# A planned attention and feed-forward kernel: new costs in the planner, masks made on GpSimd, another order of the first loads, fewer idle products

## The chip, the core and the metric

The kernel runs on one core of one Trainium2 chip. The metric is the device time of one execution in microseconds (us). Names of engines: PE is TensorE (PEld its weight loads), DVE is VectorE, ACT is ScalarE, POOL is GpSimd, SP is SyncE, on whose queue every DMA of this kernel is issued.

## What is computed

Attention over 4 batches and 8 heads, 768 positions, 64 columns a head, with a window of 128 keys and the first 4 keys (sinks) always visible, then a feed-forward layer on the 3072 rows:

```python
scores = scale * np.matmul(q, k.transpose(0, 1, 3, 2))
keep = (pos[None, :] < n_sink) | ((rel >= 0) & (rel < window))
scores = np.where(keep, scores, -1e9)
a = np.exp(scores - np.max(scores, axis=-1, keepdims=True))
a = a / (np.sum(a, axis=-1, keepdims=True) + 1e-09)
x = np.matmul(a, v)                  # then heads side by side: 3072 x 512
h = x @ w_in                         # 512 x 2048
g = np.where(h > 0, h, np.exp(np.minimum(h, 0)) - 1)
out = g @ w_out                      # 2048 x 512
```

## The kernel before

**Tiles.** The 3072 rows are 24 tiles of 128, cut into nine chunks (`SIZES`): three of 2 tiles, then six of 3. One *visit* is one tile of queries with one pair of heads, so a chunk of 2 tiles has 8 visits, and visits are counted here from 0 through chunk 0 (0 to 7), chunk 1 (8 to 15), chunk 2 (from 16). A visit of the first tile of a batch sees one tile of keys (132 columns with the sinks), any other visit two (264).

**A visit.** *Scores* (PE, line 601 in the first three chunks, in f32; 595 and 596 later), *reduction* (DVE, 616: mask added and the row's minimum taken), *Exp* (ACT, 618, with the sum read back by an accumulator instruction), the small *eps* step (622, on POOL or ACT), reciprocal (DVE, 623). In chunk 0 then: a diagonal (POOL, 630), a *turn* on PE (636), its copy out of PSUM (640, on DVE or ACT) and the *values* product (PE, 653). From chunk 1 on: two f16 halves of the weights (ACT 668, DVE 669, the sinks on POOL 675 to 679), a DMA transpose (687), and the values product (701, 706). After the visits of a pair of heads, x is copied out of PSUM in two halves (the *x copy*: ACT 739, DVE 740). There is one PSUM bank for the values products, so the next pair's wait for the x copy.

**Feed-forward.** For each of 16 column blocks f: the *first product* (PE, 765, 12 matmuls), Exp on ACT (773), two steps of the elu (775 on DVE or POOL, 776 on DVE), a rounding copy on ACT (779), the rounding rest on POOL (786), and the *second product* (PE, 793). `PARTS` cuts chunk 0's blocks in two: first chunk 0 with f 0 to 6, then chunk 1 with f 0 to 12, then the rests. The first product of chunk 1 needs all four x copies of that chunk, the eighth counted from the start.

**Weights.** There are 32 pieces (2f for the first product, 2f+1 for the second). Each is loaded (314), opened on ACT (307) and DVE (308), rounded on ACT (456), and its rest is taken on POOL in two halves (457). They are converted while the first chunks run.

**The order.** Nothing is ordered by hand. `Plan` (line 104) holds tasks with an engine, a duration, a latency after it (`HOP`, and `lat` for DMAs) and the tasks they depend on. PE's tasks have a position; `backward` gives the others a due time, `forward` fills every engine by due time, and after `ROUNDS` rounds the best order is kept; `keep_order` then issues the instructions in it. So the durations given to `add` are what decides which instruction stands before which on ACT, DVE, POOL and SP. Each of these engines, and each queue, works in the order given, so an instruction that waits holds up those behind it.

**Idle products.** Where the plan sees PE idle for over `IDLE_LEAST` in its first `IDLE_UNTIL` us, `with_idle_products` puts matmuls in, whose result nothing reads (line 882; 29 of them).

**The start.** `spread` (1109) brings the two numbers n_sink and window to every partition by a product on PE (1111); `make_masks` (326) makes distances by an iota on POOL and four steps on DVE, then the masks (345, 348). The loads stand in the order n_sink, window, first keys, first values, second keys (1125 to 1136).

Of the kernel before, what the change touches and what calls it, by code (L numbers as in the profile page):

```python
# [52 lines left out]
IDLE_US, IDLE_FILL, IDLE_UNTIL, IDLE_LEAST = 0.11, 0.6, 100.0, 0.8  # L53
# [3 lines left out]
PE_T, PE_V = 0.25, 0.25  # L57
# [46 lines left out]
class Plan:  # L104


    HOP = {"PE": 0.15, "ACT": 0.08, "DVE": 0.08, "POOL": 0.2, "SP": 0.0}
# [176 lines left out]
def act_us(n, scaled=False):  # L284
    return 0.17 + 0.00088 * n + (0.08 if scaled else 0.0)


def dve_us(n):
    return 0.12 + 0.00115 * n


def pool_us(n):
    return 0.18 + 0.0019 * n
# [32 lines left out]
def make_masks(nc, tmp, sk, low, m0, m1, m2):  # L326


    ri = tmp[:, 0:P].bitcast(I32)
    rel, own, prev = (tmp[:, i * P : (i + 1) * P] for i in (1, 2, 3))  # L330
    nc.gpsimd.iota(ri, pattern=[[-1, P]], base=0, channel_multiplier=1)
    for j in range(NS):
        nc.gpsimd.memset(sk[:, j : j + 1], float(j))
# [32 lines left out]
def fast_path(tc, ctx, first, kq, vx, wt, out, low, spread, numbers, flag):  # L366
# [36 lines left out]
    spread(po_ps[0])  # L403
# [4 lines left out]
    tmp = pts[-1].rearrange("p b k -> p (b k)").bitcast(F32)  # L408
    second, rest = make_masks(nc, tmp[:, : 4 * P], tmp[:, 4 * P : 4 * P + NS], low, m0, m1, m2)
    nc.gpsimd.memset(ones, 1.0)  # L410
    for t in wu:
        nc.gpsimd.memset(t, 0)
    nc.gpsimd.memset(hot, 1.0)
    make_identity(nc, ident)
# [11 lines left out]
    second_ = add("DVE", 0.65, second)  # L426
    rest_ = add("DVE", 0.5, rest)
    numbers_ = add("DVE", 1.3, numbers)
# [12 lines left out]
    def weights(k):  # L441
# [3 lines left out]
        ld = add("SP", 0.4, lambda: load_weights(nc, raw, wt[k]), deps=[w_done.get(k - AHEAD, [None])[0]], lat=1.45)  # L445
        if wide:
            steps = weight_f32(nc, v, top, raw, 2.0)
            a = add("ACT", act_us(512), steps[0], deps=[ld])
            b = add("DVE", 0.13 + 0.00108 * 512, steps[1], deps=[a], slow=1.5)
# [45 lines left out]
    def attention(c):  # L495
# [12 lines left out]
        def split_keys(h):  # L508
# [4 lines left out]
            if c < DUP:  # L513
                ld = None
                if (c, h) not in first["kq"]:
                    ld = add("SP", 0.4, lambda: nc.sync.dma_start(st[:, :kw], kq[:, o : o + kw]), lat=dma_us(P * kw * 4) * 1.15)
                users = []
                return st, None, ld, ld, users
# [51 lines left out]
        for p in range(NP):  # L570
# [5 lines left out]
            for g in ts:  # L576
# [29 lines left out]
                else:  # L606
                    scs = [add("PE", 0.65, scores([0, 1]), deps=kqp[0][2:4], pos=at[k], line=1)] * 2
# [6 lines left out]
                for e in range(2):  # L614
                    ee, me = e3[:, e, :wd], mn[:, e : e + 1]
                    red = add("DVE", 0.24 + 0.001 * wd, lambda ee=ee, me=me, sp=sps[e], m=m, wd=wd, to_score=to_score: nc.vector.tensor_tensor_reduce(ee, sp[:, :wd], m[:, :wd], to_score, 3.0e38, ALU.add, ALU.min, me), deps=[scs[e], (None, second_)[t] if t < 2 else rest_])  # L616
# [263 lines left out]
    for writer, users in later:  # L880
        writer.deps.extend(users)
# [290 lines left out]
```

## Time and profile before

| | us |
|---|---|
| median of 3 executions | 627.38 (626.61 to 627.97) |
| the profiled execution | 628.19 |
| its span, first to last instruction | 626.3 |
| PE busy | 606.1 (97%) |
| first product of the feed-forward, start | 32.69 |
| first product of chunk 1, start | 67.06 |
| last product of PE, end | 619.8 |

A table of stretches shows how full each engine is where; the timeline of an engine shows single steps; the table of waits says who held up whom.

### The profile page before, as it was taken

The page shows a single profiled execution, that of the slowest core. Times are in us where ns is not written, and L with a number is a line of the kernel's source. Part 1 is how long each engine was busy: PE and PEld are TensorE (multiplying, and loading weights), DVE is VectorE, ACT ScalarE, POOL GpSimd, SP SyncE. Part 2 cuts the span into 40 slices and gives each one's busy share as a digit, 9 for nine tenths or more (in the row PEclk, how much of TensorE's full clock was granted, in tenths as well). Part 3 has the DMA queues.
Part 4 walks back from the last instruction along what each step waited for, and adds up shares of the span by engine and source line. Part 5 has one row for each costly group of instructions (what it writes and reads, how often), then busy time and mean ns, then how long its engine had stood idle before and what let it go on. Part 6 is the DMA issues. An engine that isn't in the chain of part 4 may idle for free.

```text
span 626.3 us, 13397 instructions
## 1 busy us (share of the span) xinstructions
PE 606.1 (97%) x4504; PEld 359.4 (57%) x4504; DVE 462.3 (74%) x1206; ACT 421.2 (67%) x1192; POOL 294.7 (47%) x595
## 2 busy tenths in 40 slices
PE   6997999999999999999999999999999999999995
PEld 4664665667675555555555555555555555555552
DVE  7877677979878786688788988788877887543323
ACT  5887888879878876676667666676767666432221
POOL 4876689875445444344344445334324444222221
PEclk9898999999999999999999999999999999999998
DMA  8698977758656665586456865676655864413101
GB/s 293 210 248 199 298 243 192 209 139 223 145 127 157 162 146 103 94 216 181 125 153 177 230 139 159 130 197 136 166 125 124 209 144 107 115 50 92 55 2 53
DMA packets 122077, 98.24 MB, mean 157 GB/s; under 512 B 98324, under 2 KB 98324, under 8 KB 122004
## 3 DMA queue, kind: packets, MB, share of 16 engines
q1 hardware_dynamic: 122004, 97.34, 60.7%
q8 instruction: 37, 0.61, 0.4%
q14 instruction: 36, 0.29, 0.2%
HBM read 66.38 MB, written 7.34 MB: 118 GB/s over the span
## 4 chain that ended last, share of the span: by engine, by line
PE 91%; POOL 3%; DVE 2%; issue 2%; DMA 1%; ACT 1%; POOLq 0%; ACTq 0%
PE acc L793 39%; PE h L765 38%; PE po L701 5%; PE s L595 2%; PE s L596 2%; PE s L601 2%; POOL w L457 1%; PE h L882 1%; PE acc L636 1%; DMA pt<-pq 1%; DMA vs<-in_vx_dram 1%; PE po L706 1%; PE po L653 0%; DVE pt L334 0%; POOL pq L630 0%
## 5 line engine op out<-in xcount | busy, mean ns | idle before, releaser
L765 PE MATMUL h<-x,w 128*128 128x384 f16 (+1 forms) x1728 | 274.9, 309 | 2.4 <-DVE g L776 2.3
L765 PEld LDWEIGHTS <-w 128*128 128x128 f16 x1728 | 168.3, 98 | 94.8 <-issue 3.2
L786 POOL TENSOR_TENSOR gl<-g,gh 128x384 f16<-128x384 f32 (+1 forms) x144 | 128.7, 894 | 157.3 <-ACT gh L779 134.2
L793 PE MATMUL acc<-w,gh 128*128 128x512 f16 x768 | 192.7, 379 | 1.0 <-POOL w L457 1.0
L773 ACT ACTIVATE g<-h 128x384 f32<-128x384 f32 (+1 forms) x144 | 65.1, 452 | 101.8 <-PE h L765 92.2
L793 PEld LDWEIGHTS <-gh 128*128 128x128 f16 x768 | 72.9, 98 | 69.4 <-issue 0.9
L793 PE MATMUL acc<-w,gl 128*128 128x512 f16 x384 | 109.2, 379 | 0.0
L669 DVE SCALAR_TENSOR_TENSOR pq<-e,st,pq 128x256 f16<-128x256 f32 (+1 forms) x176 | 95.1, 571 | 13.0 <-ACT pq L668 12.7
L618 ACT ACTIVATE e<-e,st 128x264 f32<-128x264 f32 (+1 forms) x192 | 92.9, 484 | 12.2 <-DVE st L616 11.2
L779 ACT ACTIVATE gh<-g 128x384 f16<-128x384 f32 (+1 forms) x144 | 69.3, 481 | 43.2 <-DVE g L776 41.5
L616 DVE CUSTOM_DVE_ANT_0 e<-s,m 128x264 f32<-128x264 f32 (+1 forms) x192 | 71.7, 405 | 26.2 <-PE s L596 19.8
L776 DVE SCALAR_TENSOR_TENSOR g<-g,h 128x384 f32<-128x384 f32 (+1 forms) x144 | 72.8, 506 | 13.2 <-POOL g L775 11.3
L668 ACT ACTIVATE pq<-e,st 128x256 f16<-128x256 f32 (+1 forms) x176 | 77.1, 482 | 5.3 <-DVE st L623 4.1
L775 POOL TENSOR_SCALAR g<-g 128x384 f32<-128x384 f32 (+1 forms) x80 | 41.5, 518 | 80.2 <-ACT g L773 79.8
L775 DVE TENSOR_SCALAR g<-g 128x384 f32<-128x384 f32 (+1 forms) x64 | 26.8, 419 | 65.7 <-ACT g L773 65.4
L793 PEld LDWEIGHTS <-gl 128*128 128x128 f16 x384 | 37.5, 98 | 46.6 <-POOL gl L786 0.9
L524 ACT ACTIVATE kq<-kqs 128x780 f16<-128x780 f32 (+1 forms) x48 | 42.7, 901 | 15.7 <-PE s L596 12.2
L457 POOL TENSOR_TENSOR w<-wv,w 128x256 f16<-128x256 f32 x64 | 49.2, 789 | 5.4 <-ACT w L456 4.7
L622 POOL TENSOR_SCALAR st<-st 128x2 f32<-128x2 f32 x84 | 21.2, 253 | 48.0 <-ACT e L618 44.1
L701 PE MATMUL po<-pt,vh 128*64 128x128 f16 x656 | 35.8, 221 | 2.6 <-DVE x L740 1.9
L618 ACT ACTIVATION_READ_ACCUMULATOR e<-e,st 128x1 f32 x192 | 36.1, 188 | 0.0
L595 PE MATMUL s<-kq 128*128 128x264 f16 (+1 forms) x144 | 34.3, 267 | 0.6 <-ACT x L739 0.6
(92 smaller groups left out, 628.8 us busy)
## 6 DMA issues: line engine op xcount, KB each, us to landing
raw<-in_wt_dram SPq DMA_DIRECT2D x32, 512.0 KB, 4.8
kqs<-in_kq_dram SPq DMA_DIRECT2D x24, 456.0 KB, 3.6
kqs<-in_kq_dram SPq DMA_DIRECT2D x24, 390.0 KB, 3.6
vs<-in_vx_dram SPq DMA_DIRECT2D x28, 256.0 KB, 3.6
out_dram<-wv SPq DMA_DIRECT2D x24, 256.0 KB, 2.6
vm<-in_kq_dram SPq DMA_DIRECT2D x24, 228.0 KB, 3.7
vm<-in_kq_dram SPq DMA_DIRECT2D x24, 195.0 KB, 3.4
vm<-in_vx_dram SPq DMA_DIRECT2D x6, 768.0 KB, 5.3
```

What stands on the lines that cost most here:

```text
L616: red = add("DVE", 0.24 + 0.001 * wd, lambda ee=ee, me=me, sp=sps[e], m=m, wd=wd, to_score=to_score: nc.vector.tensor_tensor_reduce(ee, sp ...
L618: ex = add("ACT", 0.47 + 0.00085 * wd, lambda ee=ee, me=me, rs=rs[:, e : e + 1]: nc.scalar.activation(ee, ee, AF.Exp, bias=me, scale=-1.0, ...
L668: a = add("ACT", act_us(nb * P, True), lambda src=src, hi=hi, re=re: nc.scalar.activation(hi, src, AF.Copy, scale=re), deps=[rr])
L669: b = add("DVE", 0.478 if nb == 2 else 0.33, lambda src=src, hi=hi, lo=lo, re=re: nc.vector.scalar_tensor_tensor(lo, src, re, hi, ALU.mult ...
L701: nc.tensor.matmul(po[e * D : (e + 1) * D, oc], vts[i][x][:, vo : vo + D], pt[:, (2 * e + part) * nb + i, :], start=new, stop=last)
L765: nc.tensor.matmul(hp[:, :n], win[:, part, d, :], xx[:, :n], start=k == 0, stop=k == 3 * ND - 1)
L773: a = add("ACT", act_us(n) + 0.18, lambda gf=gf, hp=hp, sums=sums: nc.scalar.activation(gf, hp[:, :n], AF.Exp, scale=1.0 / G_SCALE, accum_ ...
L775: b = add("DVE", 0.14 + 0.00057 * n, lambda gf=gf: nc.vector.tensor_scalar(gf, gf, -1.0, G_SCALE, ALU.add, ALU.mult), deps=[a], slow=2.1, ...
L776: b = add("DVE", dve_us(n), lambda gf=gf, hp=hp: nc.vector.scalar_tensor_tensor(gf, gf, 0.0, hp[:, :n], ALU.min, ALU.max), deps=[b])
L779: th = add("ACT", act_us(n), lambda gf=gf, gh=gh: nc.scalar.activation(gh[:, :n], gf, AF.Copy), deps=[b])
L786: tls.append(add("POOL", pool_us(cut), lambda gl=gl, gf=gf, gh=gh, cut=cut: nc.gpsimd.tensor_tensor(gl[:, :cut], gf[:, :cut], gh[:, :cut], ...
L793: nc.tensor.matmul(acc[i], gg[:, i * P : (i + 1) * P], wout[:, part, :], start=f == f0 and k == 0, stop=f == f1 - 1 and k == 2)
```

## The change

All costs in the planner are replaced: durations become mostly shorter, latencies of most engines longer. Masks: the distances are made by two float iotas and one select on POOL, without DVE. `spread` converts the two numbers on ACT. The first keys' load is issued ahead of n_sink and window. Idle products planned before 12 us (`COLD_UNTIL`) are counted at twice their duration, so there are half as many. The eps step is always on POOL from chunk 3 on. The masks for the second and later tiles come after the first reductions, and the eight small steps of `numbers` after the first Exp of the feed-forward. The places of the branch hints on ACT move (110 to 125).

```diff
-IDLE_US, IDLE_FILL, IDLE_UNTIL, IDLE_LEAST = 0.11, 0.6, 100.0, 0.8
+IDLE_US, IDLE_FILL, IDLE_UNTIL, IDLE_LEAST, COLD_UNTIL = 0.11, 0.6, 100.0, 0.8, 12.0
-    HOP = {"PE": 0.15, "ACT": 0.08, "DVE": 0.08, "POOL": 0.2, "SP": 0.0}
+    HOP = {"PE": 0.2, "ACT": 0.14, "DVE": 0.125, "POOL": 0.09, "SP": 0.0}
 def act_us(n, scaled=False):
-    return 0.17 + 0.00088 * n + (0.08 if scaled else 0.0)
+    return 0.085 + 0.000855 * n + (0.095 if scaled else 0.0)
...
-    ri = tmp[:, 0:P].bitcast(I32)
-    nc.gpsimd.iota(ri, pattern=[[-1, P]], base=0, channel_multiplier=1)
-    nc.vector.tensor_copy(rel, ri)
-    nc.vector.tensor_scalar(own, rel, 0.0, 1.0e6, ALU.is_lt, ALU.mult)
-    nc.vector.tensor_tensor(own, own, rel, ALU.add)
-    nc.vector.tensor_scalar(prev, rel, float(P), None, ALU.add)
+    nc.gpsimd.iota(own, pattern=[[-1, P]], base=0, channel_multiplier=1, **exact)
+    nc.gpsimd.affine_select(out=own, in_=own, compare_op=ALU.is_ge, fill=1.0e6, base=0, pattern=[[-1, P]], channel_multiplier=1)
+    nc.gpsimd.iota(prev, pattern=[[-1, P]], base=P, channel_multiplier=1, **exact)
...
+                    if c == 0 and k < 2 and e:
+                        (second_, rest_)[k].deps.append(red)
-                rr = add("ACT", 0.22, ..., or_=("POOL", 0.2, ...))
+                if c < DUP:
+                    rr = add("ACT", 0.18, eps[0], deps=[ex for _, ex in exps], or_=("POOL", 0.21, eps[1]))
+                else:
+                    rr = add("POOL", 0.21, eps[1], deps=[ex for _, ex in exps])
-                tr = add("SP", 1.4, ..., lat=0.1 + 0.122 * nblk)
+                tr = add("SP", 1.4, ..., lat=0.187 * nblk)
...
+    numbers_.deps.append(exps_done[0])
-HINTS = dict(PE=8, ACT=110, DVE=120, SP=50)
+HINTS = dict(PE=8, ACT=125, DVE=120, SP=50)
+            us = IDLE_US if t.start > COLD_UNTIL else 2 * IDLE_US
...
-            nc.vector.tensor_copy(t[0:1, :], ints[0:1, :])
+            nc.scalar.activation(t[0:1, :], ints[0:1, :], AF.Copy)
-        nc.sync.dma_start(ints[0:1, 0:2], n_sink.bitcast(I32))
-        nc.sync.dma_start(ints[0:1, 2:4], window.bitcast(I32))
             nc.sync.dma_start(first[n][i][:, :w], src[:, o : o + w])
+            if n == "kqs" and i == 0:
+                nc.sync.dma_start(ints[0:1, 0:2], n_sink.bitcast(I32))
+                nc.sync.dma_start(ints[0:1, 2:4], window.bitcast(I32))
```

**Place 1: PE at the start, before.** `s` are the banks of scores, `hot` the operand of the idle products, `acc` a turn's bank. Seven and nine pairs of rows with `hot` stand where one does here.

```order
L1111 MATMUL po_172<-words,one 128x4
L601 MATMUL s_170<-kqs_63 128x132
L601 MATMUL s_171<-kqs_63 128x132
L882 LDWEIGHTS hot
L882 MATMUL h_168<-hot 128x240
...
L601 MATMUL s_170<-kqs_63 128x264
L601 MATMUL s_171<-kqs_63 128x264
...
L601 MATMUL s_170<-kqs_64 128x132
L601 MATMUL s_171<-kqs_64 128x132
L636 MATMUL acc_173<-pq_104,e_95 128x128 x2
```

The same place after the change:

```order
L1116 MATMUL po_172<-words,one 128x4
L598 MATMUL s_170<-kqs_61 128x132
L598 MATMUL s_171<-kqs_61 128x132
L598 MATMUL s_170<-kqs_61 128x264
L598 MATMUL s_171<-kqs_61 128x264
L886 LDWEIGHTS hot
L886 MATMUL h_168<-hot 128x240
...
L598 MATMUL s_170<-kqs_62 128x132
L598 MATMUL s_171<-kqs_62 128x132
L639 MATMUL acc_173<-pq_104,e_95 128x128 x2
```

The seven products between the scores of visits 0 and 1 are gone, and two stand where nine stood between visits 1 and 2. Further on six, seven, four, five and seven follow (31 in all).

**Place 2: ACT at the start, before**, with what each row waits for (`DMAHW` is a load, `DVE`, `PE`, `Pool` and `Activation` an engine):

```order
L618 ACT_TABLE_LOAD
L618 ACTIVATE e_95,st_98<-e_95,st_98 128x132 [waits DVE_49] x2
L549 ACTIVATE vh_79<-vs_66 128x512 [waits DMAHW5_49]
L618 ACTIVATE e_96,st_99<-e_96,st_99 128x264 [waits DVE_49] x2
L307 ACTIVATE wu_128<-raw_130 128x512 [waits DMAHW6_49,Pool_49]
```

After the change:

```order
L1115 ACT_TABLE_LOAD [waits DMAHW2_49]
L1115 ACTIVATE words<-words 1x4 [waits DMAHW1_49]
L617 ACTIVATE e_95,st_98<-e_95,st_98 128x132 [waits DVE_49] x2
L621 ACTIVATE st_98<-st_98 128x2 [waits Activation_49]
L617 ACTIVATE e_96,st_99<-e_96,st_99 128x264 [waits DVE_49] x2
L546 ACTIVATE vh_79<-vs_64 128x512 [waits DMAHW5_49]
L617 ACTIVATE e_97,st_100<-e_97,st_100 128x132 [waits DVE_49] x2
L643 ACTIVATE pt_107<-acc_173 128x256 [waits PE_49]
```

The table load, which waited for nothing, now stands behind the load of window; eps steps and copies of turns (643) come onto ACT.

**Place 3: POOL at the weights of blocks 9 and 10, before.** `w_136` is piece 0, so `w_155` is piece 19 and `w_157` piece 21; `gl` is the rounding rest of a block.

```order
L786 TENSOR_TENSOR gl_118<-g_114,gh_115 128x256
L457 TENSOR_TENSOR w_158<-wv_126,w_158 128x256 x2
L675 TENSOR_TENSOR st_99<-e_96,st_99 128x8
L678 CAST pq_105<-st_99 128x2x8
L679 TENSOR_TENSOR pq_105<-st_99,pq_105 128x8
L457 TENSOR_TENSOR w_155<-wv_127,w_155 128x256 x2
L786 TENSOR_TENSOR gl_119<-g_113,gh_116 128x256
```

After the change:

```order
L789 TENSOR_TENSOR gl_120<-g_114,gh_117 128x256
L454 TENSOR_TENSOR w_155<-wv_127,w_155 128x256 x2
L454 TENSOR_TENSOR w_157<-wv_125,w_157 128x256
L789 TENSOR_TENSOR gl_118<-g_113,gh_115 128x256
L454 TENSOR_TENSOR w_157<-wv_125,w_157 128x256
L454 TENSOR_TENSOR w_158<-wv_126,w_158 128x256 x2
```

Counted from the start of POOL's order, piece 19 stood behind 16 rounding rests and now stands behind 12; piece 25, the last that chunk 1's first part needs, stood behind 20 and now behind 15; the last of all 32 stood behind 28 and now behind 20.

## Rows read from the trace of the kernel before

**Rows 1.** The page: busy us of each engine over the span.

```profile
PE 606.1 (97%) x4504; PEld 359.4 (57%) x4504; DVE 462.3 (74%) x1206; ACT 421.2 (67%) x1192; POOL 294.7 (47%) x595
```

**Rows 2.** Stretches: from:to, length, busy us (instructions) per engine, clock, DMA.

```profile
5.00:32.70 27.70, 25.64 (x175) 17.09 (x174) 22.09 (x89) 21.45 (x63) 17.91 (x33) 0.94 0.77 259
32.70:67.00 34.30, 28.75 (x259) 17.89 (x258) 26.22 (x78) 28.41 (x83) 25.15 (x53) 0.95 0.95 245
67.00:112.00 45.00, 43.97 (x339) 28.32 (x339) 32.78 (x73) 38.11 (x107) 37.42 (x68) 1.00 0.77 236
200.00:619.90 419.90, 419.82 (x2981) 235.67 (x2979) 303.59 (x759) 258.63 (x719) 159.29 (x318) 1.00 0.55 134
```

**Rows 3.** Timeline of PE: start, duration, line, tile, count [idle before].

```profile
5.73 1.58 PE L882 MATMUL h<-hot 128*128 128x240 bf16 x7
7.24 1.25 PE L601 MATMUL s<-kqs 64*128 64x264 f32 x4
8.42 1.98 PE L882 MATMUL h<-hot 128*128 128x240 bf16 x9
10.33 0.81 PE L601 MATMUL s<-kqs 64*128 64x132 f32 x4
11.81 0.72 PE L601 MATMUL s<-kqs 64*128 64x264 f32 x4
...
32.69 2.79 PE L765 MATMUL h<-x,w 128*128 128x256 f16 x24
...
67.06 1.16 PE L765 MATMUL h<-x,w 128*128 128x256 f16 x9
```

**Rows 4.** Timelines of SP, ACT and DVE at the start.

```profile
1.13 0.22 SPq L1126 DMA_DIRECT2D words<-in_window_dram  x1
...
0.74 1.28 ACT L618 ACT_TABLE_LOAD   x1 [0.74 <-PEq L1163]
6.95 0.41 ACT L618 ACTIVATE e<-e,st 128x132 f32<-128x132 f32 x1 [4.93 <-DVE st L616]
...
4.20 0.15 DVE L1110 CAST words<-words 1x4 f32<-1x4 int32 x1
5.09 0.16 DVE L1112 COPY words<-po 128x4 f32<-128x4 f32 x1 [0.74 <-PE po L1111]
6.22 0.48 DVE L345 TENSOR_SCALAR m<-pt,words 128x128 bf16<-128x128 f32 x2
6.62 0.29 DVE L616 CUSTOM_DVE_ANT_0 e<-s,m 128x132 f32<-128x132 f32 x1
```

**Rows 5.** Timeline of ACT: the eighth x copy.

```profile
65.31 0.36 ACT L739 ACTIVATE x<-po 128x256 f16<-128x256 f32 x1
```

**Rows 6.** ACT's groups of instructions, 5 to 67 us: count, busy, mean ns, idle before.

```profile
L618 ACT ACTIVATE e<-e,st 128x264 f32<-128x264 f32 x26 | 13.0, 502 | 2.1 <-DVE st L616 2.1
L307 ACT ACTIVATE wu<-raw 128x512 f16<-128x512 bf16 x14 | 10.6, 770 | 2.9 <-DMA raw<-in_wt_dram 2.9
L456 ACT ACTIVATE w<-wv 128x512 f16<-128x512 f32 x14 | 8.7, 624 | 1.9 <-DVE wv L308 1.7
L668 ACT ACTIVATE pq<-e,st 128x256 f16<-128x256 f32 x16 | 7.1, 494 | 0.7 <-DMA pt<-pq 0.7
L618 ACT ACTIVATION_READ_ACCUMULATOR e<-e,st 128x1 f32 x33 | 6.2, 188 | 0.0
```

**Rows 7.** Waits, 32.7 to 67 us: who waited for whom, us in total, times, longest.

```profile
DVE e L616 <- PE s L601: 2.9, 2, 2.5
ACT wu L307 <- DMA raw<-in_wt_dram: 2.3, 1, 2.3
```

**Rows 8.** Waits of PE, 60 to 200 us.

```profile
PE acc L793 <- POOL w L457: 1.0, 2, 0.6
```

**Rows 9.** The stretch of 3.3 us in which the clock was low a second time.

```profile
52.50:55.80 3.30, 3.30 (x16) 1.96 (x14) 0.48 (x2) 2.63 (x10) 1.85 (x7) 0.52 1.03 227
```

**Rows 10.** The page: the group of POOL that takes the weights' rests.

```profile
L457 POOL TENSOR_TENSOR w<-wv,w 128x256 f16<-128x256 f32 x64 | 49.2, 789 | 5.4 <-ACT w L456 4.7
```

More of the change, by code (lines that the diff above doesn't have):

```diff
@@ L402, in fast_path @@
     hot = pool.tile([P, 2 * P], BF16, name="hot")
-    spread(po_ps[0])
     m0 = pool.tile([P, KW], BF16, name="m0")
@@ L408, in fast_path @@
     tmp = pts[-1].rearrange("p b k -> p (b k)").bitcast(F32)
+    spread(po_ps[0])
     second, rest = make_masks(nc, tmp[:, : 4 * P], tmp[:, 4 * P : 4 * P + NS], low, m0, m1, m2)
-    nc.gpsimd.memset(ones, 1.0)
+    nc.gpsimd.memset(hot, 1.0)
+    make_identity(nc, ident)
     for t in wu:
         nc.gpsimd.memset(t, 0)
-    nc.gpsimd.memset(hot, 1.0)
-    make_identity(nc, ident)
+    nc.gpsimd.memset(ones, 1.0)
     for t in pqs:
@@ L424, in slot @@
         return turn[name] % RINGS[name]
-    second_ = add("DVE", 0.65, second)
-    rest_ = add("DVE", 0.5, rest)
-    numbers_ = add("DVE", 1.3, numbers)
+    second_ = add("DVE", 0.55, second)
+    rest_ = add("DVE", 0.4, rest)
+    numbers_ = add("DVE", 1.1, numbers)
     nc1, nc2 = len(SIZES) * NF, (2 * len(SIZES) - DUP) * NP
@@ L444, in weights @@
         top = wu[k % RINGS["wu"]]
-        ld = add("SP", 0.4, lambda: load_weights(nc, raw, wt[k]), deps=[w_done.get(k - AHEAD, [None])[0]], lat=1.45)
+        ld = add("SP", 0.4, lambda: load_weights(nc, raw, wt[k]), deps=[w_done.get(k - AHEAD, [None])[0]], lat=1.5)
         if wide:
             steps = weight_f32(nc, v, top, raw, 2.0)
-            a = add("ACT", act_us(512), steps[0], deps=[ld])
-            b = add("DVE", 0.13 + 0.00108 * 512, steps[1], deps=[a], slow=1.5)
+            a = add("ACT", 0.64, steps[0], deps=[ld])
+            b = add("DVE", 0.61, steps[1], deps=[a], slow=1.5)
             ring("wu", [a], [b])
@@ L606, in attention @@
                 else:
-                    scs = [add("PE", 0.65, scores([0, 1]), deps=kqp[0][2:4], pos=at[k], line=1)] * 2
+                    scs = [add("PE", 0.7 if nb == 2 else 0.45, scores([0, 1]), deps=kqp[0][2:4], pos=at[k], line=1)] * 2
                 for kk, sc_ in zip(kqp, scs):
@@ L772, in feed_forward @@
             sums = es_of[:, c * NF + f : c * NF + f + 1]
-            a = add("ACT", act_us(n) + 0.18, lambda gf=gf, hp=hp, sums=sums: nc.scalar.activation(gf, hp[:, :n], AF.Exp, scale=1.0 / G_SCALE, accum_out=sums), deps=[s1])
+            a = add("ACT", 0.13 + 0.00091 * n, lambda gf=gf, hp=hp, sums=sums: nc.scalar.activation(gf, hp[:, :n], AF.Exp, scale=1.0 / G_SCALE, accum_out=sums), deps=[s1])
             exps_done.append(a)
-            b = add("DVE", 0.14 + 0.00057 * n, lambda gf=gf: nc.vector.tensor_scalar(gf, gf, -1.0, G_SCALE, ALU.add, ALU.mult), deps=[a], slow=2.1, or_=("POOL", 0.2 + 0.00098 * n, lambda gf=gf: nc.gpsimd.tensor_scalar(gf, gf, -1.0, G_SCALE, ALU.add, ALU.mult)))
+            b = add("DVE", 0.06 + 0.00057 * n, lambda gf=gf: nc.vector.tensor_scalar(gf, gf, -1.0, G_SCALE, ALU.add, ALU.mult), deps=[a], slow=2.1, or_=("POOL", 0.155 + 0.00084 * n, lambda gf=gf: nc.gpsimd.tensor_scalar(gf, gf, -1.0, G_SCALE, ALU.add, ALU.mult)))
             b = add("DVE", dve_us(n), lambda gf=gf, hp=hp: nc.vector.scalar_tensor_tensor(gf, gf, 0.0, hp[:, :n], ALU.min, ALU.max), deps=[b])
@@ L906, in with_idle_products @@
         if t.start - free > IDLE_LEAST and ready < free + IDLE_LEAST:
-            extra[i] = [Task("PE", IDLE_US, product, (nxt.bank,), [], 0.0, None, 1.0) for _ in range(int(IDLE_FILL * (t.start - begin) / IDLE_US))]
+            us = IDLE_US if t.start > COLD_UNTIL else 2 * IDLE_US
+            extra[i] = [Task("PE", us, product, (nxt.bank,), [], 0.0, None, 1.0) for _ in range(int(IDLE_FILL * (t.start - begin) / us))]
         free = t.start + t.dur
@@ L923, in keep_order @@
     seen = len(bb.instructions)
-    prev = {}
+    prev = {ins.engine: ins.name for ins in bb.instructions if ins.engine == E.PE}
     base = tc.cur_priority
```

44 lines of the change are left out of this document (22 added, 22 removed).

## The prediction

> **What bounds the kernel now.** I read the busy times first, then the table of stretches, then single steps. PE is busy for 97% of the span [rows 1], but not evenly. From 200 us to its last product it has 0.1 us free in 420 [rows 2]: no schedule can shorten that part, and the 6.4 us behind it are a copy, a store and the end of the program, which the change leaves alone. What can move lies ahead of 112 us. There the table shows PE free for 27.7 - 25.64 = 2.1 us before the first product of the feed-forward (32.69), 5.6 us from there to the first product of chunk 1 (67.06), and 1.0 us up to 112 us [rows 2, 3]. Before about 5 us nothing has arrived. So the question is when chunk 1's first product starts, how much of PE's work has been done by then, and what holds PE afterwards.
>
> Busy PE is not all useful PE. Between the scores of visits 0 and 1 stand 7 unread products, 1.58 us, and between visits 1 and 2 another 9, 1.98 us, 0.22 us each [rows 3]. The second group is in the way: the scores of visit 2 start at 10.33, when it ends, though the reductions they need began soon after visit 1's scores ended at 8.49. The clock matters too: the same scores of 264 columns take 1.25 us at 7.24 and 0.72 at 11.81 [rows 3], the lower of the two levels (1.2 GHz) before and the higher (2.4 GHz) after. In one later stretch of 3.3 us the granted clock is again 0.52 [rows 9].
>
> **The start, step by step.** The chain before: the two numbers are cast on DVE at 4.20, the product spreads them, their copy is at 5.09, masks follow, and the first reduction is at 6.62 [rows 4].
>
> *Moving the cast to ACT adds a wait that the diff does not show.* The order has ACT's table load, 1.28 us, behind the load of window (place 2). Before, it ran at 0.74 and cost nothing [rows 4], because nothing had arrived yet. Behind it in ACT's queue now stand the cast and with it the whole start. Window's load was issued at 1.13 and had landed by 4.20, since the cast did not wait for it [rows 4]; now it is issued one load later, at about 1.53, so it lands between 1.75 (its issue's end) and 4.60. I take 3.5, near the later end, because the keys' load now runs ahead of it in the same queue. Then 3.5 + 1.28 + about 0.2 for the cast (the smallest ACT row, 0.19 [rows 6]) is 4.98, against 4.35 before: 0.6 us later. The bounds are 1.1 us earlier and 1.7 later.
>
> *Masks.* Four 128-column masks and a small step leave the stretch between copy and first reduction (1.53 us). At 0.24 us each, half of the pair at 6.22 [rows 4], that is 1.0 us. Making the distances on POOL is hidden: POOL has until about 5 us. First reduction: 6.62 + 0.6 - 1.0 = 6.2, 0.4 us earlier. The earlier issue of the first keys gains nothing by itself, since their scores stand behind the spread on PE. The eight steps of `numbers` leave DVE at a place where it waits for PE's scores, and go to a place near 35 us: 1 us of DVE there at most, hidden beside ACT, which is fuller.
>
> *Fewer products.* Visit 1's scores follow the first reductions by 0.62 us (6.62 to 7.24), so they start near 6.8 and end near 8.1. Two products (0.45 us) fit into the time in which visit 1 is reduced, so visit 2's scores can start near 8.7 instead of 10.33: 1.6 us gained.
>
> *What is late next.* ACT. Up to the fourth x copy, which lets the feed-forward begin, ACT's order now has two more weight roundings, one more opening, three more copies of turns and three more eps steps, less two Exps: about 2.8 us more by the durations of [rows 6], 0.6 us for each big copy. ACT has 27.7 - 21.45 = 6.3 us free there [rows 2], most of it at the very start. I carry 0.7 us of the 1.6 to the first feed-forward product: 32.0.
>
> **The middle, to chunk 1's first product.** Two of the waits are of the kind that better costs remove. ACT stands 2.3 us before an opened weight whose load had not landed, and DVE stands 2.5 us before scores that PE had queued behind other work [rows 7]. Against them stands more work: up to the eighth x copy ACT's order has, compared with before, three more Exps with their reads, two more halves of attention weights, an opening, a rounding, two value copies, a rounding copy, three copies of turns and four eps steps. By [rows 6] (0.69 for an Exp with its read, 0.49 for small copies, 0.77 and 0.6 for the 512-column ones, 0.19 for eps) that is 8.6 us. From 5 to 67 us ACT is busy for 49.9 of 62 us; 2.0 of the rest is ahead of its first Exp at 6.95 [rows 2, 4], which leaves 10.2 us of gaps. The eighth x copy ended at 65.7 [rows 5]. With every gap filled it would end at 65.7 - 10.2 + 8.6 - 0.4 (the earlier start) = 63.7; with none filled, at 65.7 + 8.6 - 0.4 = 73.9. Fill-in work goes where ACT had nothing to do, so I take a value close to the first: 63.9, 1.8 us earlier, with the 0.7 us of the start in it.
>
> Of this 0.7 us is not a gain: PE's order has 19 visits scored before chunk 1's first product, where it had 20, and one visit's scores take 0.7 us [rows 3], which PE now does later, in a stretch in which it is full.
>
> **After 67 us.** PE waits 1.0 us for weight rests on POOL [rows 8], in all 1.2 with the restart of its queue. These rests now stand four or five blocks earlier in POOL's order (place 3), so the wait should go: 1.2 us gained. The price is two to three more pieces between blocks 7 and 17, at 2 x 0.789 us each [rows 10], some 4 us more on POOL, beside which it has 45 - 37.4 = 7.6 us free [rows 2].
>
> Branch hints, the eps step's engine in later chunks and the order after 200 us I cost at nothing: PE is full there and hides 100 us and more of idle time on ACT, DVE and POOL; if that cover went, one eps step on POOL instead of ACT would cost its 0.2 us.
>
> **Sum.** -1.8 + 0.7 - 1.2 = -2.3 us on the profiled execution's 628.19, thus 625.9. That execution lay 0.8 us above the median, so on the median of 627.38 I forecast **625.1**.
>
> **Rivals.**
>
> *All the slack goes.* The chain to chunk 1 runs without the two waits of [rows 7] (-4.8), the start keeps its 1.6, PE's wait for weights goes (-1.2), one visit's scores come back (+0.7): -6.9, thus 620.5. For it: ACT, DVE and POOL each have at least 17% free from 5 to 67 us [rows 2]. Against it: ACT's 8.6 us more.
>
> *Nothing comes of it.* What the start gains is taken by ACT, as the eighth x copy comes out at 65.4, and only the weights' wait goes: -0.3 + 0.7 - 1.2 = -0.8, thus 626.6. For it: in [rows 7] engines wait on one another, and behind each of these waits the next can stand.
>
> *Slower: ACT becomes the bound ahead of chunk 1.* Its order is fuller by 8.6 us. If only half of that falls into gaps, the eighth x copy is 4.3 - 0.4 = 3.9 us late; with the 0.7 and the -1.2 that is +3.4, thus 630.8. It decides for slower as soon as less than about 6.5 of the 8.6 us fall into gaps. For it: much of ACT's idle time came as waits for loads and for DVE [rows 6], and those may stay. Against it: the added work is of the kind that depends on nothing near.
>
> *Slower: the clock.* With 14 of 16 early products gone PE may stay at the lower level. The row: PE's scores fell from 1.25 to 0.72 us after a stretch in which scores and products had followed each other closely [rows 3]. If the low level lasted to the first feed-forward product, six scores of 264 columns would cost 0.53 more each and four turns of two key tiles about as much, 5.3 us less the 2.1 us that PE has free: +3.2 against the sum, thus 628.3. The Trainium skill (TensorE: Matmul & The Clock Gate, Part 1) says that "the default state is throttled, and activity releases the throttle"; by that rule taking the products out speaks against the change, and the time would be this one. By the row alone the outcome is open: at the lower level the useful matmuls themselves last twice as long and fill much of the same stretch, and seventeen products stand between visits 4 and 11 to keep PE working.
>
> That the change does nothing is not possible, as every engine's order differs.
>
> **Chances and numbers.** The forecast's case (623.5 to 626.1) has 0.45, all slack 0.20, nothing 0.15, ACT 0.14, clock 0.06. A measurement of this kernel can tell about 0.2%, 1.25 us, from no change. So faster 0.65, same 0.15, slower 0.20. The range leaves out half of the case of all slack and half of ACT's: 620.5 to 629.5. The likeliest case's own range is 623.5 to 626.1.
>
> **What would show it.** Right: the table load at 3 to 4 us with the first reduction near 6.2; visit 2's scores near 8.7; the first feed-forward product at 31 to 32.5; the eighth x copy at 63 to 65; no wait of PE for line 454. Wrong: chunk 1's first product after 68 (then the eighth x copy says whether ACT was full up to it), scores of 264 columns that still take 1.25 us at 15 us, or a wait of PE for POOL's rounding rests between 67 and 112 us.

## The result and the profile after

The change made the kernel slower: 631.08 us (630.88 to 631.55) against 627.48 us (626.61 to 627.97), four runs each; ratio 1.006, 95% interval 1.0046 to 1.0075. The forecast was 625.1, range 620.5 to 629.5: wrong in sign, and the time lies outside the range.

| | before | after | forecast |
|---|---|---|---|
| profiled execution; its span | 628.19; 626.3 | 631.26; 629.5 | |
| first reduction | 6.62 | 6.78 | 6.2 |
| scores of visit 2 | 10.33 | 9.04 | 8.7 |
| first product of the feed-forward | 32.69 | 34.99 | 32.0 |
| eighth x copy, end | 65.7 | 66.4 | 63.9 |
| chunk 1: first product | 67.06 | 66.21 | earlier by 1.8 |
| chunk 1: first product of its 13th block (f = 12) | 102.21 | 105.09 | |
| between these two | 35.15 | 38.88 | |
| last rest of a weight on POOL, end | 134.4 | 114.9 | earlier |

The stretches of the kernel after, with the columns of [rows 2]:

```profile
5.00:32.70 27.70, 23.88 (x145) 16.47 (x147) 19.50 (x71) 22.33 (x65) 17.99 (x29) 1.00 0.78 284
32.70:67.00 34.30, 31.58 (x298) 19.82 (x295) 31.38 (x95) 33.34 (x101) 28.16 (x57) 1.00 1.05 240
67.00:112.00 45.00, 41.63 (x319) 26.37 (x317) 37.39 (x72) 40.01 (x105) 43.95 (x65) 1.00 0.85 258
...
200.00:623.10 423.10, 422.99 (x3000) 237.62 (x2998) 310.29 (x766) 255.85 (x706) 166.44 (x329) 1.00 0.56 131
```

From 67 to 112 us PE has 2.3 us less work than in [rows 2], and POOL is busy for 43.95 of 45 us where it had 37.42. (The clock column counts time ahead of the trace's first clock record as full speed: the 1.00 of the first row says nothing of the time before about 17 us.) PE's waits from 60 to 200 us:

```profile
PE h L768 <- DVE g L779: 2.5, 3, 1.0
PE acc L796 <- POOL gl L789: 0.5, 1, 0.5
PE acc L796 <- ACT sv L819: 0.4, 1, 0.4
```

The wait for weights of [rows 8] is gone. In its place PE waits for the elu (779) and once for a rounding rest (789). PE's timeline (line 639 is a turn), with the 13th product of before ahead of it for comparison:

```profile
102.21 1.48 PE L765 MATMUL h<-x,w 128*128 128x256 f16 x12
```

```profile
11.35 1.25 PE L598 MATMUL s<-kqs 64*128 64x264 f32 x4
12.53 2.07 PE L639 MATMUL acc<-pq,e 128*128 128x128 f32 x8
...
17.10 1.16 PE L639 MATMUL acc<-pq,e 128*128 128x128 f32 x8
...
66.21 1.64 PE L768 MATMUL h<-x,w 128*128 128x256 f16 x12
...
91.25 1.47 PE L768 MATMUL h<-x,w 128*128 128x256 f16 x12 [0.95 <-DVE g L779]
...
105.09 1.47 PE L768 MATMUL h<-x,w 128*128 128x256 f16 x12 [1.00 <-DVE g L779]
```

**Useful work.** To see where a kernel falls behind I weighted each product that is read with the time it takes where PE is full (591.0 us in all by my weights, the same for both kernels) and compared what is done at a given time. After against before: level at 15 us, 3.1 us behind at 30, 0.4 ahead at 55, level at 65 and 70 (+0.1, -0.1), then 1.8 behind at 75, 3.7 at 95, 4.0 at 115, and 3.1 from 300 us to the end. The late start is made up; the loss is made between 70 and 115 us.

What fills POOL there, in the groups of that stretch, before:

```profile
L457 POOL TENSOR_TENSOR w<-wv,w 128x256 f16<-128x256 f32 x26 | 20.3, 801 | 0.7 <-ACT w L456 0.7
L308 DVE SCALAR_TENSOR_TENSOR wv<-raw,wu 128x512 uint32<-128x512 uint32 x12 | 11.3, 949 | 2.5 <-POOL w L457 1.4 <-ACT wu L307 1.2
L775 DVE TENSOR_SCALAR g<-g 128x256 f32<-128x256 f32 x11 | 5.7, 519 | 2.2 <-ACT g L773 2.1
```

and after:

```profile
L454 POOL TENSOR_TENSOR w<-wv,w 128x256 f16<-128x256 f32 x33 | 28.0, 867 | 0.2
L308 DVE SCALAR_TENSOR_TENSOR wv<-raw,wu 128x512 uint32<-128x512 uint32 x17 | 16.1, 947 | 3.8 <-ACT wu L307 3.4 <-POOL w L454 0.3
L778 DVE TENSOR_SCALAR g<-g 128x256 f32<-128x256 f32 x10 | 6.0, 597 | 1.8 <-ACT g L776 1.7
```

Weights take 7.7 us more of POOL and 4.8 us more of DVE. A single opening took as long before (949 ns, now 947); there are five more. Matched piece by piece in POOL's and PE's timelines, the rests of pieces 14 to 31 ended, before, from 0.9 us after to 10 us ahead of the start of the block's product that first reads them; after, 7.6 to 27 us ahead. How that holds PE up shows at 91.25, in the timelines of POOL and DVE:

```profile
89.60 2.88 POOL L454 TENSOR_TENSOR w<-wv,w 128x256 f16<-128x256 f32 x3
...
84.12 0.68 DVE L547 SCALAR_TENSOR_TENSOR vl<-vs,vh 128x512 f16<-128x512 f32 x1
84.73 0.28 DVE L778 TENSOR_SCALAR g<-g 128x256 f32<-128x256 f32 x1
...
89.03 0.75 DVE L778 TENSOR_SCALAR g<-g 128x256 f32<-128x256 f32 x1
89.71 1.16 DVE L547 SCALAR_TENSOR_TENSOR vl<-vs,vh 128x512 f16<-128x512 f32 x1
90.79 0.41 DVE L779 SCALAR_TENSOR_TENSOR g<-g,h 128x256 f32<-128x256 f32 x1
```

Two DVE steps ahead of the elu's last one take 0.75 and 1.16 us beside POOL's rests and took 0.28 and 0.68 a few us earlier: together 0.95 us longer, and PE stands for 0.95. At 72.35, where PE waits 0.60 us, the elu's first step is on POOL itself, behind two rests.

### The profile page after: what moved, and what is told of

Read it like the earlier page. It is cut to its first block, busy times and chain, and to the rows that moved or that the text cites. A ratio compares the mean times of both kernels' runs of the same rounds, so it can differ in the third digit from the quotient of the medians.

```text
span 629.5 us, 13375 instructions
## 1 busy us (share of the span) xinstructions
PE 607.6 (97%) x4506; PEld 359.4 (57%) x4506; DVE 466.3 (74%) x1204; ACT 421.9 (67%) x1190; POOL 301.1 (48%) x594
## 4 chain that ended last, share of the span: by engine, by line
PE 83%; POOL 6%; ACT 4%; DVE 3%; issue 2%; DMA 1%; SPq 0%; POOLq 0%; DVEq 0%; ACTq 0%
PE acc L796 36%; PE h L768 35%; PE po L704 4%; POOL w L454 3%; PE s L592 2%; PE s L593 2%; POOL gl L789 1%; ACT wu L307 1%; DMA raw<-in_wt_dram 1%; ACT e L617 1%; PE s L598 1%; DVE wv L308 1%; PE acc L639 1%; ACT w L453 1%; DVE e L613 1%
## 5 line engine op out<-in xcount | busy, mean ns | idle before, releaser
L789 POOL TENSOR_TENSOR gl<-g,gh 128x384 f16<-128x384 f32 (+1 forms) x144 | 124.0, 861 | 173.7 <-ACT gh L782 152.7
L672 DVE SCALAR_TENSOR_TENSOR pq<-e,st,pq 128x256 f16<-128x256 f32 (+1 forms) x176 | 102.2, 612 | 16.2 <-ACT pq L671 16.0
L778 DVE TENSOR_SCALAR g<-g 128x384 f32<-128x384 f32 (+1 forms) x70 | 28.6, 408 | 60.9 <-ACT g L776 60.7
L454 POOL TENSOR_TENSOR w<-wv,w 128x256 f16<-128x256 f32 x64 | 53.4, 851 | 4.6 <-ACT w L453 4.2
L522 DVE SCALAR_TENSOR_TENSOR kq<-kqs,kq 128x396 f16<-128x396 f32 (+1 forms) x48 | 32.4, 675 | 4.4 <-ACT kq L521 3.9
```

The source lines that it names most:

```text
L454: tls = [add("POOL", pool_us(256), lambda c=c: nc.gpsimd.tensor_tensor(w[k][:, 1, c], v[:, c], w[k][:, 0, c], ALU.subtract), deps=[th]) fo ...
L672: b = add("DVE", 0.396 if nb == 2 else 0.265, lambda src=src, hi=hi, lo=lo, re=re: nc.vector.scalar_tensor_tensor(lo, src, re, hi, ALU.mul ...
L778: b = add("DVE", 0.06 + 0.00057 * n, lambda gf=gf: nc.vector.tensor_scalar(gf, gf, -1.0, G_SCALE, ALU.add, ALU.mult), deps=[a], slow=2.1, ...
L789: tls.append(add("POOL", pool_us(cut), lambda gl=gl, gf=gf, gh=gh, cut=cut: nc.gpsimd.tensor_tensor(gl[:, :cut], gf[:, :cut], gh[:, :cut], ...
```

## The experiments

Theory W: the new costs let the planner convert weights far too early, POOL is full from 67 to 112 us, and the elu comes late. Rivals: the start (S, S1; theory C says that the start costs nothing), the added dependencies (D), the luck of one order (L). Ratios are to the kernel before on the same chip, with 95% intervals; the three last columns are of one profiled execution each. "A" is the start of chunk 1's first product, "B" the time from it to the 13th.

| run | us | ratio | A | B | POOL 67 to 112 |
|---|---|---|---|---|---|
| before | 627.5 | | 67.06 | 35.15 | 37.4 |
| after | 631.08 | 1.0060 (1.0046 to 1.0075) | 66.21 | 38.88 | 43.95 |
| old_costs | 632.84 | 1.0064 (1.0045 to 1.0083) | 71.08 | 36.39 | 38.3 |
| new_costs | 627.51 | 1.0014 (0.9991 to 1.0038) | 61.59 | 37.54 | 43.9 |
| products | 631.69 | 1.0052 (1.0040 to 1.0065) | 67.02 | 38.93 | 43.9 |
| start_only | 627.87 | 1.0013 (0.9995 to 1.0031) | 65.84 | 35.21 | 37.4 |
| old_start | 631.03 | 1.0051 (1.0038 to 1.0064) | 63.65 | 38.93 | 44.2 |
| late_weights2 | 649.86 | 1.0361 (1.0341 to 1.0381) | 66.45 | 53.20 | 22.6 |
| new_costs_late | 637.12 | 1.0149 (1.0132 to 1.0165) | 63.72 | 42.48 | 32.5 |
| after_no_rests | 626.24 | 0.9977 (0.9964 to 0.9990) | 65.82 | 34.89 | 18.5 |
| before_no_rests | 625.65 | 0.9964 (0.9953 to 0.9975) | 66.13 | 34.39 | 19.1 |
| new_costs_hold6 | 626.21 | 0.9974 (0.9958 to 0.9990) | 63.64 | 37.97 | 39.8 |
| new_costs_full | 625.52 | 0.9976 (0.9954 to 0.9999) | 66.02 | 35.13 | 37.0 |
| new_costs_deps | 630.94 | 1.0051 (1.0036 to 1.0066) | 65.12 | 38.90 | 44.1 |
| new_costs_nudge205 | 634.13 | 1.0081 (1.0053 to 1.0109) | 68.71 | 38.66 | 43.0 |
| after_full | 628.94 | 1.0016 (1.0004 to 1.0029) | 69.55 | 35.99 | 36.5 |
| full_start | 628.76 | 1.0011 (0.9996 to 1.0026) | 66.49 | 35.35 | 36.7 |
| full_nudge19 | 629.10 | 1.0012 (0.9994 to 1.0030) | 70.96 | 35.22 | 32.9 |
| full_hold6 | 626.39 | 0.9979 (0.9961 to 0.9997) | 65.20 | 34.90 | 40.6 |

Executions of one kernel differ by up to some 4 us in most rows (old_start 628.76 to 632.20, new_costs 626.41 to 633.38), and the profiled ones of these two and of full_start were their fastest, those of old_costs and full_nudge19 among their slowest; A must not be read finer than that. The four runs with the latest A (old_costs, full_nudge19, after_full, new_costs_nudge205) are also the four in whose profiled execution the granted clock was at 0.50, the lower level, for over 3 us shortly ahead of A or across it, as here in full_nudge19 and after_full:

```profile
69.10:72.40 3.30, 3.30 (x16) 1.76 (x14) 2.42 (x9) 2.52 (x8) 0.68 (x1) 0.50 1.13 284
63.30:70.00 6.70, 6.32 (x46) 3.86 (x46) 6.20 (x18) 6.67 (x22) 5.20 (x10) 0.50 1.07 284
```

PE had waited just before both (2.2 us up to 68.23, 1.1 us up to 62.16). So a late A is in part the clock, and whether the order brings that about in every execution was not tested.

**Taking the change apart.** *old_costs*: every cost as before, all else changed.

```diff
-    HOP = {"PE": 0.2, "ACT": 0.14, "DVE": 0.125, "POOL": 0.09, "SP": 0.0}
+    HOP = {"PE": 0.15, "ACT": 0.08, "DVE": 0.08, "POOL": 0.2, "SP": 0.0}
...
```

> All edits of the change but its costs: the planner keeps the costs of before. Theory W (the new costs let the planner convert weights 8 to 25 us earlier than before; POOL is then full from 67 to 112 us, and the steps of the elu come late to PE there): the weights fall back to where they were, POOL has some 37 us of work from 67 to 112 us as before, and the time is 626 to 628. Theory S (the start, with the cast on ACT behind its table load, the first keys first and fewer unread products, is what was lost; by 30 us PE was 3 us of useful work behind): the time stays above 629.5.

B is nearer to before's, as W says, but A is 4 us later, and the kernel is as slow as the change. By W this was a miss, and the time is where theory S wanted it; why this order reaches A late was not followed further.

*new_costs*: the other way round, before with the costs alone.

> The kernel before, with nothing but the new costs in its planner: start, masks, order of the first loads and unread products as before. Theory W: the costs alone bring the early weights and with them the loss: 629.5 to 631.5, POOL at 42 us or more from 67 to 112. Theory S: 626.5 to 628.

Each was half right: the time is S's, POOL is W's. PE was 4.4 us of useful work ahead of before at 70 us, and of these 3.3 were gone at 110:

```profile
67.00:112.00 45.00, 41.45 (x321) 26.22 (x320) 36.40 (x72) 40.60 (x112) 43.91 (x59) 1.00 0.87 238
```

The stretch shows W's loss in full (PE and POOL as after), and the total hides it behind a gain made earlier.

*products*: `COLD_UNTIL` 12.0 becomes 0.0.

> The changed kernel with its unread products before 12 us counted as before, so that the full number stands between the first scores; the order of all else is the same. Theory W: the start's delay is made up by 65 us anyway, so the time stays within 0.8 us of 631.1. Theory S, in its form that the clock is the cause: TensorE is at its higher clock by about 12 us as before, the first product of the feed-forward starts 1.5 to 2.5 us earlier than 34.99, and the time falls by 1 to 3 us.

Not the number of products: no time comes back, and the first feed-forward product is at 35.49. As a test of the clock the run falls short, since eight matmuls of turns still took 2.07 us at 12.81, as in the change. *start_only* puts the new start (cast, order of loads, masks, fewer products) into before's order:

> The kernel before with its own plan and costs, and of the change only what stands outside the plan: the cast on ACT, the order of the first loads, the masks on POOL, half of the early unread products, PE's order chained from the start on. Theory S1 (the new start is itself slow and its delay stays): 630 or more. Theory C (the loss of the change lies in what its plan does with the new costs and dependencies, and the new start is worth what its first reduction says, 0.2 us later or nothing): 626.5 to 628.5, with chunk 1's first product within 1 us of 67.06.

Theory C by the time; chunk 1's first product came 1.2 us early, just outside what C allowed. *old_start* takes that start out of the change:

> The changed kernel with its own plan, costs and dependencies, and the start of before in what stands outside the plan: cast on DVE, n_sink and window loaded first, masks on DVE and POOL, the full number of early products. Theory S1: the time falls to 628 or below. Theory C: it stays at 630 to 632, and POOL still has 43 us or more of work from 67 to 112 us.

Theory C again: in these two orders nothing outside the plan matters by more than can be measured. The two runs also answer the clock. In start_only scores of 264 columns still took 1.25 us at 12.01, and the time did not rise; in old_start they took 0.72 us at 10.77, and the time did not fall.

**Moving the weights.** *late_weights* and *late_weights2* shift tasks of the changed kernel's finished plan.

```diff
...
+    for k in range(14, NW):
+        use = min(u.start for t in pieces[k][2:] for u in t.succ if u.eng == "PE")
+        by = max(use - max(t.start + t.dur for t in pieces[k][2:]) - 7.0, 0.0)
+        for t in pieces[k]:
+            at[t] += by
...
```

> The changed kernel with the openings, roundings and rests of pieces 14 to 31 put back until each is ready about 7 us ahead of its first use in the plan, as in the run late_weights, but their loads left where they were, so that no opening waits for a load that was issued late. Theory W (early weights crowd POOL from 67 to 112 us): the useful work that PE has done stays level with before's from 70 to 115 us, 627 to 628.5. If the weights are not the cause: 630.5 to 631.5. If putting them back starves PE of weights in place of the elu: above 632, with waits of PE for rests of weights.

A miss that still says something. Up to 85 us the kernel stays level with before (-0.2 us; after: -1.8), as W wants. Then loads come late, in the waits from 67 to 150 us:

```profile
PE h L769 <- DVE g L780: 18.3, 6, 11.3
...
ACT wu L307 <- DMA raw<-in_wt_dram: 10.8, 2, 6.5
```

SP's queue shows why: it stood from 80.24 to 84.61 before a transpose whose operands were not ready, with a load of weights behind it. (A load also waits in the plan for the rounding of the piece five before it, so loads came later although the edit leaves them out.)

```profile
79.91 0.33 SPq L536 DMA_DIRECT2D vs<-in_vx_dram  x1
84.61 1.28 SPq L691 DMA_TRANSPOSE pt<-pq  x1
86.00 0.55 SPq L314 DMA_DIRECT2D raw<-in_wt_dram  x1
```

So this finished plan could not be shifted in part, with its loads in a queue with others'. late_weights (loads shifted as well) was 645.94 us for the same reason, and *new_costs_late*, the same edit on new_costs, failed likewise; none of the three decides about W:

> The kernel before with the new costs alone (the run new_costs, whose PE was 4.4 us of useful work ahead of before's at 70 us and lost 3 us of that up to 115), with the same putting back of pieces 14 to 31. Theory W: the lead is kept, 622 to 624.5. If the weights are not the cause: 626 to 628, as the run new_costs.

**Taking POOL's load away.** The order is kept; the rests of pieces 14 to 31 are not computed, and the products read the rounded weights in their place. PE has as many matmuls as before. The rounded weights then count twice in these blocks' sums, which is more than the loss of exactness that the expectation speaks of.

```diff
-lambda c=c: nc.gpsimd.tensor_tensor(w[k][:, 1, c], v[:, c], w[k][:, 0, c], ALU.subtract)
+lambda c=c: nc.gpsimd.tensor_tensor(w[k][:, 1, c], v[:, c], w[k][:, 0, c], ALU.subtract) if k < 14 else None
...
-                        nc.tensor.matmul(hp[:, :n], win[:, part, d, :], ...)
+                        nc.tensor.matmul(hp[:, :n], win[:, part if f < 7 else 0, d, :], ...)
...
-                        nc.tensor.matmul(acc[i], gg[:, i * P : (i + 1) * P], wout[:, part, :], ...)
+                        nc.tensor.matmul(acc[i], gg[:, i * P : (i + 1) * P], wout[:, part if f < 7 else 0, :], ...)
```

> The changed kernel in its own order, with the rests of pieces 14 to 31 on POOL left out; the products that would read them read the rounded weights in their place, so PE does the same amount of work and the output is less exact. Theory W (POOL, full from 67 to 112 us with these rests, makes the elu late and slows DVE beside it): POOL has some 17 us of work in that stretch, the useful work of PE there falls back by less than 1 us against before's in place of 3.9, and the time is 627 to 628.5, about 3.3 below 631.1. If POOL's load is not what costs time there: 630 to 631.5.

> The kernel before with the same rests left out, as the control of the run after_no_rests. Theory W: only the waits of PE for rests of weights go, 1.0 us at most: 626 to 627.5, so the gain is at least 2 us smaller than in the changed kernel. If POOL's load costs both alike: the same gain in both.

Without the rests the change gains 631.08 - 626.24 = 4.8 us and before 627.75 - 625.65 = 2.1: of the 3.6 us between the kernels 2.7 go with POOL's load. Both gained more than was expected. The control's 2.1 us, where W allowed 1.0, say that POOL's load costs something in the kernel before as well; the difference is above the 2 us that W asked for. B falls from 38.88 to 34.89, by 4.0; in the control by 0.8. From 67 to 112 us in the changed kernel without the rests:

```profile
67.00:112.00 45.00, 44.84 (x345) 29.06 (x344) 31.82 (x80) 42.18 (x116) 18.48 (x37) 1.00 0.92 274
```

and its groups there:

```profile
L308 DVE SCALAR_TENSOR_TENSOR wv<-raw,wu 128x512 uint32<-128x512 uint32 x17 | 11.8, 696 | 4.3 <-ACT wu L307 4.0
L778 DVE TENSOR_SCALAR g<-g 128x256 f32<-128x256 f32 x12 | 4.8, 400 | 5.1 <-ACT g L776 5.0
L672 DVE SCALAR_TENSOR_TENSOR pq<-e,st,pq 128x256 f16<-128x256 f32 x9 | 4.2, 496 | 0.0
```

PE is full, and the same 17 openings take DVE 696 ns in place of 947. For this stretch W stands.

**Letting the planner put the weights later.** *new_costs_hold6* has one rule more: an opening of pieces 14 to 31 isn't ready until 6 us ahead of its due time.

```diff
...
+            if t.hold:
+                ready[t] = max(ready[t], t.due - t.hold)
...
+        a.hold = 6.0 if k >= 14 else None
```

> The kernel before with the new costs alone, and one rule more in its planner: the opening of pieces 14 to 31 is not begun until 6 us ahead of its due time, so that the planner itself puts loads, openings and rests later. Theory W: a part of the 3 us that new_costs lost from 80 to 115 us is kept: 624 to 626.5. If the weights' place is not the cause: 626.5 to 628.

The time is in W's range, but B is 37.97, no shorter than in new_costs (37.54), and POOL is at 39.8: that the stretch gained is not shown here.

*new_costs_full* tells the planner two durations as the crowded stretch has them:

```diff
-tls = [add("POOL", pool_us(256), ...
+tls = [add("POOL", 0.86, ...
...
-            b = add("DVE", 0.61, steps[1], deps=[a], slow=1.5)
+            b = add("DVE", 0.95, steps[1], deps=[a], slow=1.5)
```

> The kernel before with the new costs, but the two costs of a weight that the trace of the changed kernel shows far longer from 67 to 112 us at their durations there: a rest on POOL at 0.86 in place of 0.63, an opening on DVE at 0.95 in place of 0.61. Theory W, in the form that the planner was told of the durations of engines that work alone: it sees POOL and DVE fuller, and the elu waits less: 624 to 627. If it only deals another order of the same worth: 627 to 630.

As W says. Both runs are faster than either kernel, by 0.25% against the kernel before. PE and POOL from 67 to 112 us in new_costs_full:

```profile
67.00:112.00 45.00, 45.00 (x349) 29.56 (x347) 36.35 (x77) 41.33 (x115) 37.00 (x57) 1.00 0.94 276
```

The same two costs in the change itself take most of its loss away (ratio 1.0016 in place of 1.0060):

> The changed kernel with the two costs of a weight at their durations of the full stretch (rest on POOL 0.86, opening on DVE 0.95), as in new_costs_full. Theory W: POOL at 40 us or less from 67 to 112, the useful work holds level there within 1 us, and 2 us or more of the change's 3.6 us go: 627 to 629. If theory D holds beside it, it stays 1 to 3 us above new_costs_full (625.5).

Time and POOL (36.5) are as W wants. It stays 3.4 us above new_costs_full, where D wanted 1 to 3: D, another order, or the 6.7 us at the lower clock up to about A can each be behind that.

**Dependencies or luck.** *new_costs_deps* adds the masks' and the numbers' dependencies to new_costs:

```diff
+                    if c == 0 and k < 2 and e:
+                        (second_, rest_)[k].deps.append(red)
...
+    numbers_.deps.append(exps_done[0])
```

> The run new_costs (the kernel before with the new costs) with the three added dependencies and nothing else. Theory D (the dependencies, by the order that they lead the planner to, take the lead that the costs alone had at 70 us): 630 to 632, near the run old_start (631.03), and PE's useful work at 70 us is 2 us or more behind that of new_costs. If the eps step's rule or the start is what differs: 626.5 to 628.

As D says: this alone is as slow as the whole change. But *new_costs_nudge205*, one latency at 0.205 in place of 0.2, is slower still (1.0081 in place of 1.0051, the intervals touching):

> The run new_costs with one cost changed by 0.005 us (the latency after PE, 0.205 in place of 0.2), from which the planner makes another order of weights and visits from about 20 us on. If single orders are luck (theory L): the time differs from 627.5 by 1.5 us or more. If the costs decide: 626.8 to 628.2. In both cases theory W wants POOL at 42 us or more from 67 to 112 us and 2 to 4 us of useful work lost there against the lead at 70 us, as long as the weights come early.

So what the dependencies do can't be told from dealing another order (L): a cost changed by 0.005 us moves the median by 6.6 us, the mean ratio by 0.7%. W's loss is there in every order made with the new costs and their short durations (B from 37.5 to 38.9), while A ranges among them from 61.59 to 68.71.

> The run new_costs_full (625.52) with the start of the change in what stands outside the plan, as in start_only, and without the three dependencies. The start was worth nothing in the order of before, so it should be worth nothing here: 624.8 to 626.5. If the start delays this order, whose first visits are otherwise the same: 627 or more.

A miss for theory C: 628.76 is in the range in which the start delays this order. Its executions go from 626.08 to 630.15, the intervals of the two ratios just overlap (from 0.9996 here, up to 0.9999 in new_costs_full), and A and B of the profiled one are close to those of new_costs_full. Whether the start costs this order anything stays open.

> The run new_costs_full with one cost changed by 0.01 us (the latency after PE, 0.19 in place of 0.2), which deals another order from about 20 us on. Theory W: whatever the order, POOL stays under 41 us and PE above 43.5 us of work from 67 to 112, and the useful work there falls back by less than 1 us; the time is 624 to 628. If new_costs_full was one lucky order (theory L): 628.5 or more, with the loss between 67 and 112 us.

Two of W's three signs hold (POOL 32.9, PE 43.77, and B is 35.22). The third does not, and the time is L's: useful work is level at 65 us, 4.7 us behind at 75 and 3.5 at 115. The loss is made where the stretch begins, with a wait of PE of 2.2 us for a transpose, up to 68.23, and the lower clock right behind it (0.50 from 69.1 to 72.4, above).

> The run new_costs_full with the rule of new_costs_hold6 beside it (pieces 14 to 31 not opened until 6 us ahead of their due time). PE was full from 67 to 112 us in new_costs_full already, so theory W has nothing more to gain there: 624.5 to 627, and any difference is made before 67 us, by the order. If early weights still cost there: 623 to 624.5.

As W says. The three best (new_costs_hold6, new_costs_full, full_hold6) lie 0.2% under the kernel before, close to what can be told, and about 0.8% under the change. Over all orders, what speaks for W is B: 34.9 to 36.0 us in the five runs that were told the long durations, 37.5 to 38.9 in the seven with the short ones (leaving aside those without rests or with weights moved in the finished plan). The times overlap (ratios 0.9976 to 1.0016 against 0.9974 to 1.0081), as what happens ahead of A differs from order to order.

## Why the prediction was wrong, step by step

**The step that failed** is the price in "After 67 us": two to three more pieces, "some 4 us more on POOL, beside which it has 45 - 37.4 = 7.6 us free". It was costed at nothing. Three things were wrong. The pieces were 3.5 (33 halves for 26), and a half took 867 ns in the mean, where it took 801 before: 7.7 us more in all, as much as was free. The openings and roundings that belong to them, five or six more on DVE and on ACT, were not counted; by themselves they cost nothing, as after_no_rests keeps them and B falls to 34.89. And free time in a sum is not free at the moment when a short step of the elu comes: it waits behind rests of 0.7 to 1.1 us, and DVE runs slower beside them. B grew by 3.7 us, 0.7 of them the scores put off, where the sum had -1.2 beside these. The sign that I had named as wrong, a wait of PE between 67 and 112 us, came, mostly one engine further on (DVE's elu, 2.5 us; rounding rests, 0.5). The gain in the same term was real, as the wait for weights went, but the term as a whole came out at a loss of 3.0 us. Without the rests B is 0.3 us below before's, with the 0.7 us of scores in it: that is the gain, some 1.0 us, without its price.

**The start.** The table load ran at 3.50, as forecast, and the copy of the two numbers out of PSUM came 0.65 us later (0.6 forecast). The masks saved 0.5 us, not 1.0, so the first reduction is 0.2 later rather than 0.4 earlier. Visit 2's scores gained 1.3 of the 1.6 us.

```profile
3.50 1.28 ACT L1115 ACT_TABLE_LOAD   x1 [3.50 <-DMA words<-in_window_dram]
4.80 0.21 ACT L1115 ACTIVATE words<-words 1x4 f32<-1x4 int32 x1
```

```profile
6.78 0.29 DVE L613 CUSTOM_DVE_ANT_0 e<-s,m 128x132 f32<-128x132 f32 x1 [0.15 <-DVE m L345]
```

The 0.7 us for the first feed-forward product was wrong by 3 us (34.99), and without consequence: PE had made it up by 55 us. In start_only the same start moved it by 0.2 us, and in old_start the changed order with the start of before has it at 32.45: neither alone delayed it, the two together did.

**The middle.** Both waits of [rows 7] are gone, and ACT is busy for 33.3 of 34.3 us there. The eighth x copy is 0.7 us later, not 1.8 earlier: the 8.6 us more on ACT did not fall into gaps only. Chunk 1's first product still came 0.85 us earlier, since PE began it with the other heads. Less the 0.7 us of scores put off, this is nothing, and useful work is level at 70 us. By size the step was off by 1 us.

**The rivals.** "Slower: ACT becomes the bound" gave 630.8, near the time, for a wrong reason: ACT was full, but it cost about 1 us. The clock stayed at the lower level (1.2 GHz) longer, as eight matmuls of turns still took 2.07 us at 12.53 and 1.16 at 17.10, after scores, turns and values products with only two unread ones; the stretch of [rows 9] did not come back, at a granted clock of 1.00, nor did an earlier one that the rows leave out (before, 0.50 from 18.2 to 21.5 us). It cost nothing that lasted: start_only is as late at the higher level and as fast as before, old_start is early at it and as slow as the change. The rule of the Trainium skill that I cited (TensorE: Matmul & The Clock Gate, Part 1) points the way that the trace went; by those two runs it had no price here. After 200 us PE is full, as said. Sum of what happened: nothing up to 70 us, +4.0 to 115, -0.9 up to 300 us: +3.1, against +3.2 in the spans.

**The range** had no case in which an order that a planner makes is simply worse by chance. The runs show several us of that, in either direction.

## What to carry to other kernels

Give a planner the durations of the stretch in which the work will run, not those of an engine left alone, and ask of work with a late due time what short step will stand behind it; here all five runs told so kept B short, though not all of them were faster. Before costing extra work on an engine at nothing, look at when it is free and who waits there, not at the sum of its free time. A single order out of a planner is one draw: compare two or three that differ by a hair before crediting a few us to an edit.

## What was not expected of the hardware

DVE's steps depend on what POOL does beside them, and on their operands. In the changed kernel the opening (308, two inputs in SBUF) lasted from 0.67 to 1.18 us from 67 to 112 us, and with POOL's rests gone, in the same order, 0.67 to 0.69 in all but one of 17. The elu's last step (779), which reads PSUM and SBUF, took 0.40 to 0.42 us in both. The Trainium skill (SBUF — State Buffer, Who interferes with whom) says that a DVE instruction with two inputs in SBUF contends with a GpSimd instruction that reads SBUF; the trace agrees. The planner knows of it (`lock`), and its short costs still left POOL no room.

Executions of one kernel differ by up to 7 us (new_costs) on one chip. Their mean granted clock goes with it: in full_start the three at 0.999 took 626.1 to 626.5 us and the four at 0.991 or 0.992 took 629.2 to 630.2, and in all kernels here but before_no_rests the slower executions tend to have the lower clock. What makes the clock differ was not settled.
